# Attention and a bilinear FFN on one core: the order of 4,367 operations from a fixed table instead of a list rule

## The chip, the cores and the metric

The kernel runs on one core of one Trainium2 chip. The metric is the device time of one execution in microseconds (us), and the figure compared is the median over several runs. The notation is that of the profile: PE is TensorE's matmul side and PEld its weight loads, DVE is VectorE, ACT is ScalarE, POOL is GpSimd, and SP is SyncE, which only issues DMAs here.

## What is computed

Eight batches of twelve heads (448 positions, head width 64) go through attention with RMS-normalised queries and keys. The result, seen as a 3584 x 768 matrix, goes through a bilinear feed-forward network. All of it is in fp32.

```python
q_n, k_n = rmsnorm(q, g_q), rmsnorm(k, g_k)
scores = scale * np.matmul(q_n, k_n.transpose(0, 1, 3, 2))
attn = softmax(scores)
x = np.matmul(attn, v).transpose(0, 2, 1, 3).reshape(B * S, H * D)
out = (x @ w_a) * (x @ w_b) @ w_out
```

## The kernel before

**Attention** is cut into 24 steps, p = 0 to 23, each of four heads of one batch (three steps make a batch). For each p, three loads bring q, k and v (SP queue). `normalize` squares q and k on ACT (L458), sums them on DVE (L460), raises the mean to the power -0.5 on POOL (L466) and scales q on DVE (L470). `transposes` turns k and q on PE (L496) into a PSUM tile, and ACT copies each result to SBUF (L501 for k, L503 for q). Then come seven slices j of the keys. `scores(p, j)` is a product on PE in 64x64 tiles (L517) followed by two exponentials on ACT (L523). `values(p, j)` multiplies them with v on PE (L539). The denominators are summed on PE: for p < 5 slice by slice (`sums_over_keys`, L575), from p = 5 on after DVE and POOL have added the slices (`add_up`, L553). `invert` copies the denominators to SBUF on ACT (L588), sends one row to 112 partitions by DMA, takes the reciprocal on DVE (L608), writes it to DRAM and reads it back spread over all partitions (three transfers on the SP queue, called few, inv and rec below), and `divide` (L646) multiplies the result with it. `put_out` (L635) moves the products out of PSUM on ACT.

**Buffers.** Scores, transposed q and k and, from p = 5 on, the denominators share two PSUM buffers, tag "sc". Exponentials have four SBUF buffers, q one, k one, v two, and the spread reciprocals one ("rec").

**The network** uses a fast matrix-product scheme of seven products per 2x2 block. Its weights are prepared at the start in 18 sets (`factors`): ACT issues two loads and takes an absolute value (L271), DVE rounds (L272 to L278) and combines (L394), ACT issues the store of the result ("keep", L401 and L405). Batches are taken in pairs, beta = 0 to 3. For beta 0 and 1, `quarter_products` makes 7 products of three matmuls each for every (m, ab) (L1202). For beta 2 and 3, `deep_products` goes one level deeper (L779). `last_product` multiplies with w_out (L903, and L1100 for the deeper form `inner_products`). On the full array a matmul in the program is two records in the trace, and so is one in 64x64 tiles: a `scores`, `values` or `sums_over_keys` operation is 8 records, a transpose operation 7, a quarter product 6, half a last product 6.

**What sets the order.** Nothing is issued while the functions above run. Each calls `op`, which records an operation in a list: its engine, a planned duration, a key (a due place: lower goes first), a function that emits the instructions, what it depends on, its PSUM or SBUF tiles, and on PE its mode, "quad" for 64x64 tiles or "full". `Plan.run` then walks through time: for each engine it finds the operations that could begin within a short window (0.2 us on PE, 0.05 us elsewhere), takes the one with the lowest key, moves that engine's clock by the planned duration, and so on. It emits the operations in the order in which they were chosen. Each engine runs its own instructions in the order in which they were emitted; waits between engines are by semaphores. The planned durations and keys therefore decide only the order.

Of the kernel before, what the change touches and what calls it, by code (L numbers as in the profile page):

```python
# [24 lines left out]

class Plan:
# [9 lines left out]
    TURN = 0.18  # L36
    LANES = 8
    RATE, LANDING = 300.0, 2.0
    STAY = 0.3
    LAG = 0.1  # L40
# [31 lines left out]
    def run(self):  # L72
        ops = self.ops
        links, first = {}, {}
        for n, o in enumerate(ops):
            if o[6] is not None:
                links.setdefault(o[6], []).append(n)
        for c in links.values():
            for n in c:
                first[n] = c[0]  # L80
        users, need, left, last = {}, {}, {}, {}
        for n, o in enumerate(ops):
            head = first.get(n, n)
            outer = {d for d in o[4] if first.get(d, d) != head}
            need[head] = need.get(head, 0) + len(outer)
            for d in outer:
                users.setdefault(d, []).append(head)
            for t in o[9]:
                left[t] = left.get(t, 0) + 1
        ready = {n: 0.0 for n in need}  # L90
        opened, free, modes, cands, dma, port = {}, {}, {}, {}, 0.0, 0.0
        for n, k in need.items():
            if k == 0:
                cands.setdefault(ops[n][0], []).append(n)

        def members(n):
            return links[ops[n][6]] if ops[n][6] is not None else [n]

        def buffers(n):

            t, taken = 0.0, {}
            for x in members(n):
                for name in ops[x][8]:
                    tag, bufs = self.tags[name]
                    had = opened.setdefault(tag, [None] * bufs)
                    since = [(last.get(o, 0.0), k) for k, o in enumerate(had) if (tag, k) not in taken.values() and not left.get(o)]
                    if not since:
                        return None
                    t, taken[name] = max(t, min(since)[0]), (tag, min(since)[1])
            return t, taken  # L110

        order, end, sent = [], {}, [0.0] * self.LANES
        while any(cands.values()):
            best = None
            for e, cs in cands.items():
                f = free.get(e, 0.0) if e else 0.0
                at = {}
                for n in cs:
                    t = buffers(n)
                    if t is not None:  # L120
                        t = t[0]
                        turn = self.TURN if ops[n][5] != modes.get(e) else 0.0
                        if e == "PE" and modes.get(e) == "quad" and turn:
                            turn += self.STAY
                        at[n] = max(f, ready[n], t, port if ops[n][10] else 0.0,
                                    sent[ops[n][11] - 1 - self.LANES] if ops[n][11] else 0.0) + turn
                if at:
                    t = min(at.values()) + (0.2 if e == "PE" else 0.05)
                    n = min((n for n in at if at[n] <= t), key=lambda n: (ops[n][2], n))
                    t = at[n] - (self.STAY if e == "PE" and modes.get(e) == "quad" and ops[n][5] != "quad" else 0.0)  # L130
                    if best is None or t < best[0]:
                        best = t, e, n
            t, e, n = best
            cands[e].remove(n)
            for name, (tag, k) in buffers(n)[1].items():
                opened[tag][k] = name
            for x in members(n):
                if ops[x][5] != modes.get(e) and x != n:
                    t += self.TURN
                modes[e] = ops[x][5]  # L140
                order.append((t, x))
                t += ops[x][1]
                end[x] = t
                if ops[x][10]:
                    port = max(port, t)
                if ops[x][7]:

                    dma = max(dma, t) + ops[x][7] / self.RATE
                    end[x] = dma + self.LANDING
                    sent += [end[x]] * ops[x][11]  # L150
                for name in ops[x][9]:
                    left[name] -= 1
                    last[name] = max(last.get(name, 0.0), end[x])
                for u in users.get(x, ()):
                    ready[u] = max(ready[u], end[x] + (self.LAG if ops[u][0] != e else 0.0))
                    need[u] -= 1
                    if need[u] == 0:
                        cands.setdefault(ops[u][0], []).append(u)
            if e:
                free[e] = t  # L160
        assert len(order) == len(ops)
        self.times = order, end
        for _, n in order:
            if ops[n][3] is not None:
                ops[n][3]()


# [3 lines left out]
def kernel(  # L171
# [35 lines left out]
    nc = tc.nc  # L207
# [91 lines left out]
    def fast_body(ld, wk, ps_s, ps_o, ps_mm, dram):  # L299
# [27 lines left out]
        def rounding(key, size, get, x, w):  # L327

            for e, n, emit, r, wr in round_steps(get):
                rate = {"ACT": 950, "DVE": 1900 if n == 1 else 950, "POOL": 420}[e]  # L330
                names = {"x": x, "w": [w]}
                op(e, 0.17 + size / rate, key, emit, sum((names[c] for c in r), []), sum((names[c] for c in wr), []),
                   lock=e != "ACT")
# [25 lines left out]
        def factors(n, key, early, after):  # L359
# [30 lines left out]
            for pool_, to, x, y in steps:  # L390
                add = to == 4 and not last
                e = FACTOR if pool_ else "DVE"
                op(e, 1.05 if e == "POOL" else 0.6, key,
                   lambda e=e, to=to, x=x, y=y, add=add: two[e].tensor_tensor(  # L394
                    sts[n][:, to], sts[n][:, x], sts[n][:, y], ALU.add if add else ALU.subtract),
                   [f"{st}/{homes[x]}", f"{st}/{homes[y]}"], [f"{st}/{homes[to]}"], lock=True)
# [44 lines left out]
        def normalize(p):  # L441
# [8 lines left out]
            def squares(s, nm):  # L450
# [8 lines left out]
                op("ACT", 1.07, key, square, [f"{nm}{p}"], [sq], new=[sq])  # L459
                op("DVE", 1.1, key, lambda: nc.vector.tensor_reduce(rs[p][:, s], xs["sq", nm, p], AX, ALU.add), [sq], [f"{ms}/{nm}"])  # L460

            def roots(a, b, names):
                msf = lambda: rs[p][:, a:b].rearrange("p s n -> p (s n)")
                op("DVE", 0.2, key, lambda: nc.vector.tensor_scalar(msf(), msf(), 1.0 / D, 1e-6, ALU.mult, ALU.add), [], names)  # L464
                op("POOL", 2.7 if b - a == 1 else 5.0, key,
# [20 lines left out]
        def transposes(p):  # L486

            qkT, key = tile_of(f"qkT{p}", "qkT", 2), p - EARLY
            for n, nm in ((1, "k"), (0, "q")):
# [17 lines left out]
                op("ACT", 1.05 if n else 1.15, key, take, [pt, "gain"], [f"{qkT}/{n}"], new=[qkT] if n else [])  # L507

        def scores(p, j):
# [17 lines left out]
            op("ACT", 1.12, p, exps, [sc, f"ms{p}/k"], [E], new=[E])  # L527
# [15 lines left out]
        def add_up(p, j):  # L543
# [10 lines left out]
            op(e, 2.2 if e == "POOL" else 1.12, p, emit, [f"E{p}.{j}"] + ([f"E{p}.0"] if j == 1 else []), [t],  # L554
# [163 lines left out]
        def deep_products(beta, key, names, h):  # L718
# [12 lines left out]
            for f, x in enumerate(xs_of):  # L731
# [4 lines left out]
                for n, a, b in ((0, lambda t=token: t(0, 1), lambda t=token: t(0, 0)), (1, lambda t=token: t(1, 1), lambda k=block: k(0)),  # L736
# [6 lines left out]
                    op("DVE", 0.32, -0.4, emit, [f"{x}/0", f"{x}/1", "ended" if beta == ONCE else f"{h}/open"] + ([nm] if n else []),  # L743
# [5 lines left out]
            def step(m, f, F, names_F):  # L749
# [21 lines left out]
                def product(nm, to, terms, reads, new=None, more=False):  # L771
# [9 lines left out]
                    op("PE", len(terms) * HS / 595, key + 0.1 * (7 * m + f), emit, reads + [slot], [nm, "ffn"],  # L781
# [19 lines left out]
                def wide(to, other):  # L801
                    take("DVE", 1.02, lambda: V.tensor_tensor(F[to], F[to], F[other], ALU.add), allF(other), allF(to), lock=True)  # L802

                def times(g, i, n):
                    e = "DVE" if m == MH - 1 and f > 4 else TIMES
                    take(e, 1.2 if e == "POOL" else 0.63,
# [19 lines left out]
                take("DVE", 0.66, lambda: V.tensor_tensor(  # L826
# [36 lines left out]
        def last_product(beta, h, key):  # L863
# [48 lines left out]
            def add(to, x, t, names_in, names_out):  # L912

                return lambda po, ps: op("DVE", 0.6, -1, lambda: nc.vector.tensor_tensor(to(), x(), ps(), ALU.add),
                                         [po] + names_in, names_out)

            def out_(t, i, x, y):
# [3 lines left out]
                def take(po, ps):  # L921
# [5 lines left out]
                    op("DVE", 0.6, -1, emit, [po, f"{fin}/{'cU'[y]}{t}"], [o_sb], new=[o_sb])  # L927
# [41 lines left out]
            def plain(t, base, to):  # L969
# [3 lines left out]
                if not isinstance(to, tuple):  # L973
                    return lambda po, ps: op("DVE", 0.6, -1, lambda: nc.vector.tensor_tensor(acc(t, to), acc(t, base), ps(), ALU.add),
                                             [po, name(base)], [name(to)])

                def take(po, ps):
                    out_(t, *to[:2], base)(po, ps)
                    if len(to) > 2:
                        op("DVE", 0.6, -1, lambda: nc.vector.tensor_tensor(acc(t, to[2]), acc(t, to[2]), ps(), ALU.add),  # L980
                           [po], [name(to[2])])
# [76 lines left out]
        def inner_products(beta, key, f, group, a, base, to, acc, names, out_place):  # L1058
# [31 lines left out]
            def product(bank, x, y, reads, start, stop):  # L1090
# [11 lines left out]
                op("PE", MI * HI / 595, key, emit, reads, [nm, "ffn"], new=new, mode="full")  # L1102
# [83 lines left out]
        def quarter_products(beta, key, m, ab, st, at, names, h):  # L1186
# [42 lines left out]
            if ab == 0:  # L1229
                take("DVE", 0.68, lambda: V.tensor_tensor(fresh("U", "U", 1), C(0, 0), PS("b"), ALU.add), [b_, hp[0]], [U], [U])  # L1230
            else:
                take("DVE", 0.68, lambda: V.tensor_tensor(fresh("U", "U", 1), held["t1"], PS("b"), ALU.add), [b_, t1], [U], [U])
# [3 lines left out]
            else:  # L1236
                take("DVE", 0.68, lambda: V.tensor_tensor(C(0, 0), C(0, 0), PS("a"), ALU.mult), [a], [hp[0]])
            d = product("d", 4, B12, True, False)
            if ab == 0:
                take("DVE", 0.68, lambda: V.tensor_tensor(C(1, 1), held["U"], PS("d"), ALU.add), [d, U], [hp[1]])  # L1240
# [251 lines left out]
```

## Time and profile before

| | us |
|---|---|
| median of 3 runs | 1521.26 (1517.19 to 1521.43) |
| the profiled execution, its own time | 1517.54 |
| its span (first to last instruction) | 1515.7 |
| PE busy | 1477.4 |
| DVE busy | 1009.6 |
| ACT busy | 441.2 |
| POOL busy | 324.7 |

Stages in the profiled execution, read off the trace by which operations PE runs: from 0 to 228 us attention p = 0 to 10 with the weights being prepared; to 380 us the first network part of beta 0 alone; to 480 us attention p = 10 to 14 between parts of beta 0; to 725 us the network of beta 0 and 1; to 920 us attention p = 15 to 23 between last products of beta 1; from 920 us to the end the network of beta 2 and 3.

A row of the windows view has the stretch and its length, and then, engine by engine, the busy time and the number of instructions; the last three figures are the granted TensorE clock as a share of full speed, the mean busy share of the DMA engines, and GB/s. A row of the timeline has the start, the duration, the engine, the line, the operation, what it writes and reads, how many records are merged, and in brackets how long the engine had been idle and what ended that. A row of the waits view has who waited for whom, the total in us, how often, and the longest.

### The profile page before, as it was taken

The numbers are of one execution on the slowest core, as the hardware profiler recorded it, in microseconds if no ns is written. First come the engines' busy times: TensorE is split into PE (matmuls) and PEld (weight loads), VectorE is DVE, ScalarE is ACT, GpSimd is POOL, SyncE is SP. The second block draws the span as 40 slices with busy tenths as digits, with TensorE's granted clock in tenths as the row PEclk, the third lists the DMA queues.
The fourth block names the chain that finished last, engine by engine and source line by source line (L and its number), as shares of the span: only waits on it lengthen the run. The fifth ranks groups of instructions, "written<-read, shape, count | busy, mean of one in ns | idle before, by whom it ended". The sixth has DMA issues, their size and how long they took to land.

```text
span 1515.7 us, 21017 instructions
## 1 busy us (share of the span) xinstructions
PE 1477.4 (97%) x7854; PEld 981.6 (65%) x7854; DVE 1009.6 (67%) x1568; ACT 441.2 (29%) x790; POOL 324.7 (21%) x172
## 2 busy tenths in 40 slices
PE   8998999999999999999999999999999999999998
PEld 5553345555445555555544445699997889999798
DVE  5887869888784233343667656477777667777785
ACT  6777661111554000000177761011111011111000
POOL 3426442111241001000265541011210001211000
PEclk9999999999999999999999999999999999999999
DMA  9897455554532464555656534655555755554554
GB/s 274 247 283 194 99 111 181 189 200 156 156 109 75 130 191 136 167 177 182 184 134 169 119 115 123 186 156 157 157 157 187 254 165 158 157 157 135 197 172 118
DMA packets 189074, 250.73 MB, mean 165 GB/s; under 512 B 61988, under 2 KB 160804, under 8 KB 182308
## 3 DMA queue, kind: packets, MB, share of 16 engines
q1 hardware_dynamic: 160900, 195.82, 45.5%
q10 hardware_dynamic: 28064, 53.48, 10.0%
q8 instruction: 64, 1.05, 0.3%
q14 instruction: 46, 0.38, 0.1%
HBM read 191.10 MB, written 57.97 MB: 164 GB/s over the span
## 4 chain that ended last, share of the span: by engine, by line
PE 86%; DMA 6%; DVE 3%; ACT 2%; issue 1%; SPq 1%; ACTq 0%; DVEq 0%
PE pq L1202 25%; PE dg L779 17%; PE po L903 15%; PE da L779 6%; PE o L539 6%; PE sc L517 6%; PE g L1100 2%; PE a L1100 2%; PE pt L496 2%; DMA q_sb<-in_q_dram 2%; PE su L575 1%; ACT ET L523 1%; PE b L1100 1%; DMA kept_o<-st 1%; PE d L1100 1%
## 5 line engine op out<-in xcount | busy, mean ns | idle before, releaser
L1202 PE MATMUL pq<-x,st 128*128 128x448 f32 x1008 | 382.4, 541 | 0.0
L1202 PEld LDWEIGHTS pq<-x,st 128*128 128x128 f32 x1008 | 190.8, 190 | 188.7 <-issue 181.7
L523 ACT ACTIVATE ET<-sc,ms 128x448 f32<-128x448 f32 x336 | 192.3, 632 | 86.5 <-PE sc L517 71.1
L539 PE MATMUL o<-ET,v_sb 64*64 64x448 f32 x1344 | 192.5, 546 | 3.6 <-ACT ET L523 2.9
L517 PE MATMUL sc<-qkT 64*64 64x448 f32 x1344 | 180.0, 543 | 16.3 <-ACT ET L523 9.1
L466 POOL TENSOR_TENSOR ms<-ms,expo 128x14 f32<-128x14 f32 x48 | 151.3, 3154 | 176.2 <-DVE ms L464 175.6
L779 PE MATMUL dg<-x,st 128*128 128x224 f32 x672 | 169.6, 355 | 2.0 <-DVE dF L826 2.0
L779 PE MATMUL dg<-dT,st 128*128 128x224 f32 x672 | 168.3, 353 | 1.9 <-DVE dt L819 1.9
L903 PE MATMUL po<-st,hT 128*128 128x384 f32 x492 | 163.4, 488 | 0.0
L807 POOL TENSOR_TENSOR hT<-dF 128x448 f32<-128x448 f32 x42 | 47.6, 1143 | 427.3 <-DVE dF L802 427.3
L903 PEld LDWEIGHTS po<-st,hT 128*128 128x128 f32 x492 | 92.9, 190 | 66.9 <-issue 6.0
L779 PEld LDWEIGHTS dg<-x,st 128*128 128x128 f32 x672 | 126.5, 190 | 5.3 <-DVE dF L826 5.3
L779 PEld LDWEIGHTS dg<-dT,st 128*128 128x128 f32 x672 | 126.7, 190 | 3.2 <-DVE dt L819 2.8
L779 PE MATMUL da<-x,st 128*128 128x224 f32 x504 | 123.2, 353 | 1.1 <-ACT dt L792 1.1
L517 PEld LDWEIGHTS sc<-qkT 64*64 64x64 f32 x1344 | 60.7, 133 | 89.6 <-issue 35.5
L539 PEld LDWEIGHTS o<-ET,v_sb 64*64 64x64 f32 x1344 | 61.3, 132 | 81.1 <-ACT ET L523 42.3
L553 POOL TENSOR_TENSOR sum<-sum,ET 128x896 f32<-128x896 f32 x38 | 81.1, 2134 | 104.0 <-ACT ET L523 60.8
L779 PEld LDWEIGHTS da<-x,st 128*128 128x128 f32 x504 | 93.0, 190 | 4.5 <-ACT dt L792 2.1
L802 DVE TENSOR_TENSOR dF<-dF 128x896 f32<-128x896 f32 x84 | 93.3, 1111 | 3.4 <-DVE dF L831 0.5
L792 ACT COPY dt<-da 128x224 f32<-128x224 f32 x84 | 29.1, 346 | 209.2 <-PE da L779 209.2
L553 DVE TENSOR_TENSOR sum<-sum,ET 128x896 f32<-128x896 f32 x57 | 62.0, 1088 | 38.2 <-POOL sum L553 34.0
L903 PE MATMUL po<-st,fin 128*128 128x384 f32 x252 | 86.7, 492 | 0.0
(136 smaller groups left out, 1683.6 us busy)
## 6 DMA issues: line engine op xcount, KB each, us to landing
st<-kept_o SPq DMA_DIRECT2D x28, 1152.0 KB
st<-kept_s SPq DMA_DIRECT2D x84, 320.0 KB
kept<-st ACTq DMA_DIRECT2D x12, 1344.0 KB
st<-kept SPq DMA_DIRECT2D x12, 1344.0 KB
st<-kept SPq DMA_DIRECT2D x84, 192.0 KB
ti<-kept_t SPq DMA_DIRECT2D x48, 288.0 KB
kept_s<-ds SPq DMA_DIRECT2D x30, 448.0 KB
q_sb<-in_q_dram SPq DMA_DIRECT2D x48, 224.0 KB
```

What stands on the lines that cost most here:

```text
L466: lambda: nc.gpsimd.tensor_tensor(msf(), msf(), expo[:, 0:2 * NT * (b - a)], ALU.pow), [], names)
L496: nc.tensor.transpose(t[:, j * P:(j + 1) * P], x[:, j].rearrange("p h d -> p (h d)"), ident)
L517: nc.tensor.matmul(t[low_high[w], e, 0:S], lhsT=qkTs[p][low_high[e], 1, j * P + w * D:j * P + (w + 1) * D], rhs=qkTs[p][low_high[e], 0, w ...
L523: nc.scalar.activation(E[:, e], scs[p, j][:, e, 0:S], AF.Exp, scale=rs[p][:, 1, 2 * j + e:2 * j + e + 1])
L539: nc.tensor.matmul(os_[p][low_high[e], w, 0:S], lhsT=xs["v", p][low_high[w], e, j * D:(j + 1) * D], rhs=ETs[p, j][low_high[w], e], start=( ...
L553: two[e].tensor_tensor(sums[p], sums[p] if j > 1 else ETs[p, 0], ETs[p, j], ALU.add)
L779: nc.tensor.matmul(to(), lhsT=W(w), rhs=t(), start=not more and k == 0, stop=k == len(terms) - 1, skip_group_check=True)
L802: take("DVE", 1.02, lambda: V.tensor_tensor(F[to], F[to], F[other], ALU.add), allF(other), allF(to), lock=True)
L807: lambda: two[e].tensor_tensor(C(i, n), F[g][:, 0:S], F[g][:, S:2 * S], ALU.mult), allF(g),
L903: nc.tensor.matmul(held["po"][:, 0:HALF], lhsT=a[0]()[:, c], rhs=sts[beta, 12 + place_of[f]][:, c], start=(c == 0), stop=(c == MH - 1))
L1100: nc.tensor.matmul(held[bank], lhsT=x()[:, c], rhs=y(c), start=(start and c == 0), stop=(stop and c == MI - 1), skip_group_check=True)
L1202: nc.tensor.matmul(banks[bank][:, 0:S], lhsT=sts[at][:, f, c * P:(c + 1) * P], rhs=quads[x][:, c], start=(start and c == 0), stop=(stop an ...
```

## The change

The body of `Plan.run` is replaced. In place of the walk through time there is a table, `ORDER`, a packed list of 4,367 places. Step k takes the operation at place `places[k]` of those not yet emitted, checks that all it depends on has been emitted, and emits it.

```diff
-            t, e, n = best
-            cands[e].remove(n)
...
-        for _, n in order:
-            if ops[n][3] is not None:
-                ops[n][3]()
+        n = len(ops)
+        places = zlib.decompress(base64.b85decode(ORDER))
+        assert len(places) == 2 * n
+        rest, at = list(range(n)), {}
+        for k in range(n):
+            x = rest.pop(places[k] + 256 * places[n + k])
+            assert all(d in at for d in ops[x][4])
+            at[x] = k
+            if ops[x][3] is not None:
+                ops[x][3]()
```

Many planned durations change too, for example

```diff
-                op("ACT", 1.07, key, square, [f"{nm}{p}"], [sq], new=[sq])
+                op("ACT", 0.95, key, square, [f"{nm}{p}"], [sq], new=[sq])
```

and so do the constants of `Plan` (`TURN` from 0.18 to 0.13, `LAG` from 0.1 to 0.04, and new ones). The new `run` reads none of them: it uses only an operation's dependencies and its emitting function. Operations, tiles, buffer counts and DMAs are the same in both kernels.

The table can be decoded and laid beside the order that the rule of before gives. How many operations stand at another place of their engine's own queue:

| engine | operations | moved | furthest, places |
|---|---|---|---|
| PE | 1450 | 343 | 10 |
| DVE | 1566 | 1176 | 39 |
| ACT | 678 | 342 | 18 |
| POOL | 164 | 93 | 15 |
| SP | 455 | 373 | 58 |

On PE every move lies in the attention stages; behind the last `sums_over_keys` (920 us in the profile) PE's order is the same. PE changes between quad and full mode 105 times in the order of before (counting the first) and 93 times in the table. As an example, PE's queue around p = 6 (S is `scores`, V `values`, U `sums_over_keys`, T a transpose of k or q, with p and j behind S and p behind the others; V's slices come in the order of S's):

```
before: S6.0 S6.1 U5 V6 S6.2 V6 S6.3 V6 S6.4 V6 S6.5 V6 S6.6 V6 Tk7 Tq7 V6 S7.0 S7.1 V7 S7.2 U6 V7 S7.3
table:  S6.0 S6.1 S6.2 V5 S6.3 U5 V6 S6.4 V6 V6 S6.5 V6 V6 S6.6 V6 Tk7 Tq7 V6 S7.0 S7.1 S7.2 S7.3 U6 V7 S7.4
```

## The prediction

> **What bounds the kernel now.** I read the page first, then busy time by stage, then PE's own waits, then PE's timeline where it stalls, last the chain of waits. The page's first part and the windows:
>
> ```profile
> PE 1477.4 (97%) x7854; PEld 981.6 (65%) x7854; DVE 1009.6 (67%) x1568; ACT 441.2 (29%) x790; POOL 324.7 (21%) x172
> ```
> ```profile
> 0.00:114.00 114.00, 104.06 (x956) 63.27 (x957) 89.29 (x108) 80.16 (x121) 40.59 (x20) 1.00 0.95 269
> 114.00:228.00 114.00, 103.12 (x799) 45.62 (x798) 83.61 (x97) 78.79 (x128) 59.59 (x24) 1.00 0.56 133
> 228.00:380.00 152.00, 152.00 (x405) 76.85 (x404) 133.61 (x155) 23.93 (x25) 26.92 (x17) 1.00 0.51 181
> 480.00:725.00 245.00, 245.00 (x680) 129.34 (x680) 87.86 (x123) 10.07 (x20) 16.95 (x15) 1.00 0.52 161
> 725.00:920.00 195.00, 191.26 (x1396) 91.96 (x1395) 131.31 (x184) 120.84 (x200) 98.93 (x39) 1.00 0.56 141
> 920.00:1516.00 596.00, 582.11 (x2926) 528.44 (x2922) 414.20 (x820) 69.66 (x199) 47.57 (x42) 1.00 0.55 167
> ```
>
> PE is the bound, at full clock. Where only the network runs (228 to 380, 480 to 725) it never stops; no order can help there. In the first 228 us it stands still 20.8 us, though DVE (76%) and ACT (70%) have room: these are waits of order, not of capacity. The DMA engines are nearly full (0.95) in the first 114 us.
>
> A stall costs more than its idle time, because a restarted matmul shows its whole latency as busy. So I summed, over PE's 7,854 records, the time from start to start less the back-to-back interval of the form. The intervals come from rows such as these of the chain:
>
> ```profile
> 227.75 158.11 PE pq L1202 x420
> 479.46 62.12 PE po L903 x192
> ```
>
> 158.11 / 420 = 0.376 us, 62.12 / 192 = 0.323 us; likewise 0.189 us for 224 columns, 0.163 for 192, 0.109 for a transpose, and 0.75 us for the eight records of a 64x64 operation. At these intervals all records take 1425.0 us; 82.9 us are **lost between starts**: 6.7 before 14 us, 14.7 to 114, 22.4 to 228, 0 to 380, 6.8 to 480, 0 to 725, 18.0 to 920, 14.3 after. How it is lost in the two attention stages:
>
> ```profile
> 73.47 1.74 PE L517 MATMUL sc<-qkT 64*64 64x448 f32 x16 [1.14 <-ACT qkT L503]
> 75.58 1.12 PE L539 MATMUL o<-ET,v_sb 64*64 64x448 f32 x5 [0.37 <-ACT ET L523]
> ```
> ```profile
> 137.18 0.93 PE L517 MATMUL sc<-qkT 64*64 64x448 f32 x8
> 137.93 0.93 PE L539 MATMUL o<-ET,v_sb 64*64 64x448 f32 x8
> 139.39 0.98 PE L517 MATMUL sc<-qkT 64*64 64x448 f32 x8 [0.52 <-ACT ET L523]
> 140.19 0.93 PE L539 MATMUL o<-ET,v_sb 64*64 64x448 f32 x8
> 141.65 0.98 PE L517 MATMUL sc<-qkT 64*64 64x448 f32 x8 [0.52 <-ACT ET L523]
> ```
>
> First row: scores wait 1.14 us for ACT's copy of the transposed q, as nothing stands between. Second: values wait for exponentials. Below: the denominators of step 5 hold one of the two "sc" buffers from 135.6 us until ACT copies them at 147.0, and scores go through the other one by one: 2.26 us a round (139.39 to 141.65) for 1.5 us of work.
>
> **The skill.** The Trainium skill, "Trainium Kernel Development and Optimization", Performance Expectations, says that matmul busy time is a bad metric for the distance to the best, as matmuls are pipelined; the trace agrees (97% busy, yet 82.9 us, 5.5%, lost). "TensorEngine Tiling (Array Packing)", Key Properties, says that changing the tiling mode drains TensorE; here the last 64x64 record to a full-array one takes 0.466 us where the next 64x64 group takes 0.354, and full to 64x64 takes 0.093 more than its interval: about 0.1 us a turn. "PSUM — Partial Sum Buffer", Engine vs sequencer instructions, says that ScalarE, VectorE and GpSimd queues are strict first in, first out: a misplaced instruction holds all behind it. "DMA: Bandwidth & Descriptors", Issuing engines are not separate DMA queues, says that transfers from all issuers share 16 engines; the trace has a q load landing after 9.30 us (issued 121.58) amid weight loads.
>
> **The change part by part.** The order is known before any run: I decoded the table and laid it beside the rule's order. From it I take positions alone; durations are the trace's.
>
> *Planned durations*: nothing, they are no longer read. *Operations, DMAs, waits*: the same number of each; no new wait exists, only other places in the queues.
>
> *Turns on PE*: 105 to 93, 12 x 0.1 = **1.2 us** gained, all on the path.
>
> *PE's places in attention.* An exponential pair is done about 1.5 us after its scores leave the array (139.39 + 0.75 to 141.65), so two 64x64 operations must stand between. I counted, over all 24 steps, places with too little between (by the intervals above): values behind their scores with less than 1.4 us of PE work: 12 before, **0** in the table. Scores that need a buffer whose exponentials had less than 1.4 us: 14 and **5**. Scores behind the q transpose with nothing between: 4 and **1**. Scores issued while denominators hold a buffer: 28 and **16**. Of 30 bare places (the first three kinds) 24 go. Values with just two operations between fall from 78 to 19: slack for ACT's queue. The cover is other attention work, or a piece of the network that was there anyway.
>
> By stage, in us:
> - 14 to 114: 14.7 lost, 0.9 of it turns (9). 6 of 8 bare places go, but this stage also waits on DMA and DVE. I take 8 of 13.8.
> - 114 to 228: 22.4, 2.0 turns (20). 10 of 14 bare places go. I take two thirds of 20.4: 13.5.
> - 380 to 480: 6.8, 2.6 turns (26): 2.5 of 4.2.
> - 725 to 920: 18.0, 4.8 turns (48). All 7 bare places go, but many small waits remain: 8 of 13.2.
> - After 920 PE's order is the same. DVE's wait-makers move: the factor of the block at 1454 us (PE waits 1.8 us) stands six places earlier in DVE's queue. The four waits near 1 us at the start and end of each deep part come from PE's own order and stay. 2 of 14.3.
> - Before 14 us: loads, the norm and POOL's power chain set it; 0.
>
> With the turns: 8 + 13.5 + 2.5 + 8 + 2 + 1.2 = **35.2 us**.
>
> *Moves on ACT, DVE, POOL and SP* (342, 1176, 93, 373 operations) are the price, not shown by this trace, so bounded: at best 0 (all work hidden behind PE); at worst they give all of it back (a rival). Queued behind a misplaced store ("keep") or denominator copy on ACT are the exponentials, and PE waits for those within 1.5 us. Counts to the same landmarks hardly differ (weight loads on ACT's queue ahead of step 5's first exponentials: 16 before, 15 in the table), so DMA pressure is the same per step but in less time. One place I can price: the first product that needs step 5's combined block (at 171 us) comes through denominators copied at 147.0, three transfers, divide and combine, done at 165.4: 18.4 us. In the table that product stands some 14 us of PE work behind the copy. I take 4 us here and 2 elsewhere: **-6**.
>
> Sum: 35.2 - 6 = 29 us. DVE must then do its 172.9 us of the first 228 in some 206: 84%, still not the bound. The profiled execution (1517.54) would become 1488; the median of the three runs is 3.7 above it. From the median: 1521.3 - 29 = **1492 us**, likeliest range 1482 to 1502.
>
> **Rivals.**
> 1. *Round trips through DMA set the pace of a step.* q has one buffer: load (9.3 us when DMA is full), square 0.95, sum 1.08, power 3.15, scaling 1.09 make 15.6 us a step before queueing, where PE's own work for p < 5 is 17.4 us (21 x 0.75 + 14 x 0.109 + turns). The denominators' trip from 170.8 to 182.4 is 11.6 us, and "rec" has one buffer. For: the chain of waits runs through these transfers. Against: PE's waits name ACT, hardly DMA (1.4 us). If they take the place of half the gain: 1521 - 14 = 1507, with 1502 to 1516.
> 2. *Slower: ACT's queue blocked by denominator copies.* The table fixes where each copy stands among the exponentials; if "rec" comes free later than its place, exponentials behind it wait, and PE with them. Price: the trace has 5.2 us of this wait in 6 places, 1.2 at most. It decides once it passes 35 / 24 = 1.5 us per step beyond what the copies cost now, in all 24 steps; at 2 us a step the kernel takes 1521 + 48 - 35 = 1534.
> 3. *Nothing*: the PE places are filled but the waits move on to exponentials, ACT being busy 70% of the first 228 us. Then 1521 within 5 us. Against: the other 30% is room. That the table does not reach the chip can't be: each engine takes emitted order.
> 4. *Better than I allow*: few new waits and three quarters of the 51 us of non-turn loss in attention go: 38 + 1.2 for turns + 2 after 920, 1521 - 42 = 1479.
>
> **How the numbers follow.** Forecast 0.50, rival 1 0.25, rival 4 0.10, nothing 0.08, slower 0.07. The measurement can tell about 0.3% (4.6 us). Faster: 0.50 + 0.10 + 0.25 = 0.85; same 0.08; slower 0.07. The range reaches up through rival 1 and down past rival 4's centre: 1476 to 1514.
>
> **What would show it.** PE's idle time in the first 228 us' worth of work falls from 20.8 to under 10 us; step 6's rounds of 2.26 us go to 1.5; waits of scores on L503 and L523 (15.2 us on PE) halve; time between starts lost in all falls to about 54 us; the stretches of pure network keep their lengths. Wrong would be: new PE waits on DMA or on DVE's combine over 10 us, longer waits of ACT's denominator copies, or the stage after 920 us changed by over 5 us.

## The result, and the profile after

The kernel with the table is slower: 1598.11 us, median of 6 runs (1594.04 to 1600.98), against 1521.05 us for the kernel before (6 runs, 1517.19 to 1522.87). The ratio is 1.0506, 95% interval 1.0488 to 1.0525. The time lies outside the predicted range, on the other side of no change.

The profiled execution after took 1594.04 us, span 1592.2. Lines of the kernel after are those of before less 32 (L779 is now L747, L819 is L787). The page's first part, then the rows of the windows for attention's start and for the part from 920 us:

```profile
PE 1489.2 (94%) x7854; PEld 953.4 (60%) x7854; DVE 980.5 (62%) x1568; ACT 438.9 (28%) x790; POOL 318.5 (20%) x172
```
```profile
0.00:114.00 114.00, 100.81 (x928) 49.00 (x928) 85.93 (x106) 78.79 (x119) 36.47 (x19) 0.99 0.90 253
114.00:228.00 114.00, 106.94 (x845) 46.57 (x842) 83.76 (x106) 81.44 (x132) 65.32 (x24) 1.00 0.58 147
920.00:1592.00 672.00, 594.49 (x2892) 517.65 (x2890) 391.64 (x796) 67.60 (x197) 46.90 (x42) 0.99 0.48 147
```

The clock is full, DVE, ACT and POOL are busy for less time than before, and PE for only 11.8 us more. The last stage is 76 us longer with 12.4 us more of busy PE: 77.5 us of idleness where there were 13.9. The first two stages hold as much idleness as before (20.3 us; it was 20.8). Because stage borders shift, I compared the start of the same PE operation in both traces:

| PE reaches | before | after | gained since the row above |
|---|---|---|---|
| values of p = 5 | 118.2 | 120.4 | -2.2 |
| values of p = 11 | 394.2 | 395.7 | 0.7 |
| values of p = 20 | 850.2 | 847.0 | 4.7 |
| first deep product, beta 2 | 972.4 | 962.4 | 6.8 |
| its last products | 1149.5 | 1188.9 | -49.4 |
| first deep product, beta 3 | 1228.9 | 1269.0 | -0.7 |
| its last products | 1405.5 | 1483.9 | -38.3 |
| end of the span | 1515.7 | 1592.2 | 1.9 |

Attention gained 10.0 us in all. The two stretches of deep products lost 87.7. PE's waits after:

```profile
PE dg L747 <- DVE dt L787: 49.5, 46, 2.3
PE dg L747 <- DVE dt L786: 8.7, 15, 1.0
PE sc L485 <- ACT qkT L471: 6.2, 7, 2.1
PE pt L464 <- ACT ET L491: 5.4, 3, 2.7
PE dg L747 <- DVE dF L794: 4.3, 12, 0.8
PE da L747 <- ACT dt L760: 4.3, 6, 1.1
PE sc L485 <- ACT ET L491: 2.9, 5, 0.6
```

And the rows of before that bear on these:

```profile
PE sc L517 <- ACT ET L523: 9.1, 15, 1.5
PE sc L517 <- ACT qkT L503: 6.1, 9, 1.2
PE dg L779 <- DVE dt L819: 1.9, 2, 1.0
```

The scores' waits for exponentials fell from 9.1 to 2.9 us. Their waits for the copy of q did not fall: three of the four longest of before are gone, but two longer ones have come, 1.45 us at 134.43 and 2.10 us at 787.34. The top two rows of after are for the two DVE additions into dt of a deep step, and before they came to 1.9 us in 2 places. For what follows, four names within a deep step, by the code printed above: the *first products* go to columns of bank 0 of the tile dg; the two *adds* (L786, L787) read them; the two *second products* go to bank 1; the *third product* accumulates into bank 1, and the *last add* (L799) reads it. One step of before and one of after in the timeline, without the rows of weight loads, ACT and DMA issues:

```profile
1057.42 0.92 PE L779 MATMUL dg<-dT,st 128*128 128x224 f32 x4
...
1058.18 0.92 PE L779 MATMUL da<-x,st 128*128 128x224 f32 x4
1058.45 0.39 DVE L818 TENSOR_TENSOR dt<-dt,dg 128x224 f32<-128x224 f32 x1 [0.48 <-PE dg L779]
1058.87 0.39 DVE L819 TENSOR_TENSOR dt<-dt,dg 128x224 f32<-128x224 f32 x1
1058.94 0.92 PE L779 MATMUL dg<-x,st 128*128 128x224 f32 x4
...
1059.69 0.54 PE L779 MATMUL dg<-dT,st 128*128 128x224 f32 x2
1059.89 0.39 DVE L831 TENSOR_TENSOR dF<-dt,dg 128x224 f32<-128x224 f32 x1 [0.63 <-PE dg L779]
```
```profile
1046.72 0.92 PE L747 MATMUL dg<-dT,st 128*128 128x224 f32 x4
...
1048.24 0.92 PE L747 MATMUL dg<-x,st 128*128 128x224 f32 x4
...
1049.19 0.39 DVE L799 TENSOR_TENSOR dF<-dt,dg 128x224 f32<-128x224 f32 x1 [1.97 <-PE dg L747]
1049.50 0.38 DVE L786 TENSOR_TENSOR dt<-dt,dg 128x224 f32<-128x224 f32 x1
...
1049.91 0.39 DVE L787 TENSOR_TENSOR dt<-dt,dg 128x224 f32<-128x224 f32 x1
...
1050.35 0.65 PE L747 MATMUL dg<-dT,st 128*128 128x224 f32 x2 [1.20 <-DVE dt L787]
```

Before, the adds run at 1058.45, while PE works on the product to da, and are done by 1059.26, ahead of the second products (1059.69). After, in the table's order the last add of the step before (L799) stands ahead of them in DVE's queue. It waits 1.97 us for the third product of its own step, so the adds, ready since about 1047.6, start at 1049.50, and PE, with its second product next, stands 1.20 us.

Why does PE wait at all? A second product reads nothing that the adds write, and it writes a bank that they don't read. In the built program of each kernel a second product waits for an add only where the add was emitted ahead of it; where the add is emitted behind it, the add waits for the product instead. The two share the tile dg, and the ordering on that tile follows the order of emission; the experiments test this. The plan names the halves of dg apart (`gb`, `gg`), so this wait is in neither its dependencies nor its model. The rule emits the adds ahead of both second products in 82 of the 84 deep steps, and early in DVE's queue. The table puts the last add of the previous step ahead of the second of the two adds in 57 of 82 neighbouring step pairs (of the first as well in 25). In 68 of the 84 steps it emits at least one add ahead of a second product, and in 16 both behind both. By start-to-start intervals (the prediction's measure of lost time) the second products lose 74.6 us (2.6 before) and the third 8.2 (3.9).

### The profile page after: what moved, and what is told of

Its sections match the earlier page's. It is cut to its first block, busy times and chain, and to the rows that moved or that the text cites. A ratio compares the mean times of both kernels' runs of the same rounds, so it can differ in the third digit from the quotient of the medians.

```text
span 1592.2 us, 21039 instructions
## 1 busy us (share of the span) xinstructions
PE 1489.2 (94%) x7854; PEld 953.4 (60%) x7854; DVE 980.5 (62%) x1568; ACT 438.9 (28%) x790; POOL 318.5 (20%) x172
## 5 line engine op out<-in xcount | busy, mean ns | idle before, releaser
L747 PE MATMUL dg<-dT,st 128*128 128x224 f32 x672 | 175.3, 363 | 58.3 <-DVE dt L787 49.5
L747 PE MATMUL dg<-x,st 128*128 128x224 f32 x672 | 169.9, 355 | 4.4 <-DVE dF L794 4.3
L434 POOL TENSOR_TENSOR ms<-ms,expo 128x14 f32<-128x14 f32 x48 | 145.6, 3037 | 133.9 <-DVE ms L432 133.5
L747 PEld LDWEIGHTS dg<-dT,st 128*128 128x128 f32 x672 | 122.7, 190 | 80.2 <-DVE dt L787 65.5
L485 PE MATMUL sc<-qkT 64*64 64x448 f32 x1344 | 157.1, 549 | 9.7 <-ACT qkT L471 6.2
L507 PE MATMUL o<-ET,v_sb 64*64 64x448 f32 x1344 | 153.4, 540 | 0.6 <-ACT ET L491 0.6
L747 PEld LDWEIGHTS dg<-x,st 128*128 128x128 f32 x672 | 125.6, 190 | 10.4 <-DVE dF L794 9.5
L747 PE MATMUL da<-x,st 128*128 128x224 f32 x504 | 125.0, 357 | 5.1 <-ACT dt L760 4.3
L485 PEld LDWEIGHTS sc<-qkT 64*64 64x64 f32 x1344 | 47.2, 133 | 95.2 <-issue 43.1
L747 PEld LDWEIGHTS da<-x,st 128*128 128x128 f32 x504 | 93.2, 191 | 12.0 <-ACT dt L760 9.6
L507 PEld LDWEIGHTS o<-ET,v_sb 64*64 64x64 f32 x1344 | 53.1, 133 | 72.1 <-issue 59.4
L786 DVE TENSOR_TENSOR dt<-dt,dg 128x224 f32<-128x224 f32 x84 | 32.4, 385 | 84.4 <-PE dg L747 84.2
```

The source lines that it names most:

```text
L434: lambda: nc.gpsimd.tensor_tensor(msf(), msf(), expo[:, 0:2 * NT * (b - a)], ALU.pow), [], names)
L485: nc.tensor.matmul(t[low_high[w], e, 0:S], lhsT=qkTs[p][low_high[e], 1, j * P + w * D:j * P + (w + 1) * D], rhs=qkTs[p][low_high[e], 0, w ...
L507: nc.tensor.matmul(os_[p][low_high[e], w, 0:S], lhsT=xs["v", p][low_high[w], e, j * D:(j + 1) * D], rhs=ETs[p, j][low_high[w], e], start=( ...
L747: nc.tensor.matmul(to(), lhsT=W(w), rhs=t(), start=not more and k == 0, stop=k == len(terms) - 1, skip_group_check=True)
L786: take("DVE", 0.38, lambda: V.tensor_tensor(part(1), part(0), bank(0, 0)(), ALU.add), [gb, tt], [tt])
```

## Experiments

Theory A is the one just given. Theory B puts the loss on DVE's queue alone, theory C on what the new attention part leaves behind when the deep part begins. In all these kernels both orders are kept as tables, `table` and `rule`, and a third is made of them; none leaves out any computation. The first, second, fourth and fifth ran on one chip beside the kernel before at 1519.08 us, the others on another beside 1517.89 us; each ratio is to the kernel before on the same chip. The first and the fourth can't tell A from B, since both expect the same there; the second and the fifth can.

**The rule's order from the first deep product on.**

```diff
+    head = head[:next(k for k, x in enumerate(head) if first in plan.names[x])]
+    there = set(head)
+    return head + [x for x in tail if x not in there]
```

Here `head` is the table, `tail` the rule's order and `first` the first deep product, "da2.0.0".

> The table's order up to the first product of the deep part (da2.0.0, 974 us in the changed kernel), the rule's order from there. Theory A (in the deep part the emitted order decides which of two engines waits: TensorE's products into the second bank of a 'dg' tile wait for VectorE's adds out of its first bank when those were emitted earlier, and the adds wait for products emitted earlier; the table puts the adds between the two products): the 85 us lost behind da2.0.0 come back, 10 us of attention gain stay: 1511 us. Rival B (VectorE's own queue order in the deep part is to blame, whatever the emitted order): the same 1511. Rival C (the deep part is late because of transfers or buffers that the attention stages left behind): most of the loss stays, above 1560.

Measured: 1510.82 us (1509.08 to 1512.69), ratio 0.9944 (0.9927 to 0.9960). C falls: the loss lies in the order from the first deep product on. The rest of the table is a gain of some 8 us, and this kernel is faster than both. Its waits in the deep part are those of before:

```profile
PE dg L801 <- DVE dF L848: 2.0, 2, 1.0
PE dg L801 <- DVE dt L841: 1.9, 2, 1.0
```

**Only the order of emission changed.** Every engine's queue is exactly that of before; the adds are emitted between the two second products.

```diff
+            before += [(second[0], adds[0]), (adds[1], second[1])]
+    return merged(plan, rule, queues_of(plan, rule), before)
```

> The rule's order: every engine's queue exactly as in the kernel before. Only the emitted order between engines differs: in each of the 84 deep steps the two adds are emitted between the two products, so that the adds wait for the first product and the second product waits for the adds. A: 84 waits of about 1 us each, 1595 to 1610 us. B and C: 1521.

Measured: 1628.95 us (1628.51 to 1634.33), ratio 1.0734 (1.0712 to 1.0756). No instruction moved in any queue, and the kernel is 110 us slower. Of all pairs of operations on different engines that share a tile, only 164 were emitted in the other order: in 82 steps the two adds and the one second product (in the first step of each deep part the rule had them so already). One step, without weight loads and ACT, and the row of the waits:

```profile
1062.40 0.54 PE L838 MATMUL dg<-x,st 128*128 128x224 f32 x2
1063.05 0.39 DVE L877 TENSOR_TENSOR dt<-dt,dg 128x224 f32<-128x224 f32 x1 [2.70 <-PE dg L838]
1063.47 0.39 DVE L878 TENSOR_TENSOR dt<-dt,dg 128x224 f32<-128x224 f32 x1
...
1063.91 0.65 PE L838 MATMUL dg<-dT,st 128*128 128x224 f32 x2 [0.97 <-DVE dt L878]
```
```profile
PE dg L838 <- DVE dt L878: 81.9, 84, 1.3
```

The wait comes in each of the 84 deep steps. The adds wait for the one second product and the other waits for the adds: two handovers in each step. Idleness is 0.98 us a time, but from start to start the second products lose 104.4 us and the third 10.5. A's mechanism holds; its size was too low, since it counted the idleness alone (1595 to 1610 us were expected). B and C can't explain this run.

**The tile declared as two.** In the kernel just shown, the buffer of every third deep step (`turn == 1`) is declared as two tiles of one bank each, in place of one of two banks.

```diff
-                            held["g"] = (ps_o if turn == 1 else ps_s).tile([P, 2, 512], FP32, tag=home[0], name="dg")
+                            held["g"] = two_banks("dg") if turn == 1 else [ps_s.tile([P, 2, 512], FP32, tag="sc", name="dg")]
...
+        def two_banks(name):
+            return [ps_o.tile([P, 512], FP32, tag=f"o{n}", name=name) for n in range(2)]
```

The other users of that buffer, attention's values among them, get the two tiles as well.

> The kernel with every queue as before and only the adds emitted between the two products (1628.95 us, every step's second product waiting for the add), with one thing changed: the buffer of 2 x 512 words that every third deep step takes is declared as two buffers of one bank each, in the same place and of the same total size. Theory A (the wait is one on the buffer as a whole, although the product writes a bank that the add doesn't read): in those 28 of 84 steps the wait is gone and in the other 56 nothing changes. In the run without the split the steps of each of the three kinds lost 35 us before that product, so 1594 us (1588 to 1600), and PE's row of waits for the second add falls from 84 times to about 56. Rival D (the two are in each other's way in the memory itself, or the order in which the operations are emitted changes something else): 1622 to 1635, and the loss of 35 us in those steps stays.

Measured: 1591.97 us (1590.45 to 1597.16), ratio 1.0500 (1.0483 to 1.0516), as A said.

```profile
PE dg L843 <- DVE dt L883: 54.7, 56, 1.3
```

28 of the 84 waits are gone, those of the split steps. By kind of step, the second products lose 35.0, 0.0 and 34.7 us, where without the split they lost 35.0, 34.7 and 34.7. So it is the declaration of the tile, not the memory, that makes PE wait. This agrees with the Trainium skill, "PSUM — Partial Sum Buffer", PSUM bank collisions raise a hardware error, whose rule in its simple version is to guard PSUM by bank. In two of the split steps a second product even runs beside an add out of the other bank, which happens in no step of the unsplit kernels; one of them:

```profile
1178.13 0.39 DVE L883 TENSOR_TENSOR dt<-dt,dg 128x224 f32<-128x224 f32 x1
1178.18 0.54 PE L843 MATMUL dg<-dT,st 128*128 128x224 f32 x2
```

**The table with the adds ahead.** In DVE's queue the adds go ahead of the last add of the previous step (`r`), and both are emitted ahead of the second products, as the rule does it.

```diff
+            if q.index(r) < q.index(adds[1]):
+                q[:] = [x for x in q if x not in adds]
+                q[q.index(r):q.index(r)] = adds
+        before += [(adds[1], second[0]) for adds, _, second in part]
```

> The table everywhere; in the deep parts alone, each step's two adds into dt move ahead of the last add of the step before where the table had them behind it (181 of VectorE's 1566 places), and are emitted ahead of both products. A and B: the waits of those products (74 us between starts) go, about 1515 to 1525 us. C: no change, 1598.

Measured: 1517.86 us (1513.33 to 1525.86), ratio 0.9993 (0.9982 to 1.0004): 80.3 us of the difference from the kernel with the table (1598.11) are back, of the 86.5 that it lost from the first deep product to the end. In the profile (of the longest of the 20 runs, 1525.86 us) PE still waits for adds in 11 places:

```profile
PE dg L842 <- DVE dt L882: 10.1, 11, 1.8
```

**The table's queues with the adds emitted late.** Every queue as in the kernel with the table; both second products are emitted ahead of the adds, so that they don't wait.

```diff
+            before += [(second[1], adds[0])]
+    return merged(plan, table, queues_of(plan, table), before)
```

> The table: every engine's queue exactly as in the changed kernel. Only the emitted order differs: in each of the 84 deep steps both products are emitted ahead of the adds, so that TensorE does not wait for the adds there, and the adds wait for both products. A: the 74 us of waits on the adds go, but the adds end later and some third products (which wait for the adds' reader) become late by some tenths of a us: 1525 to 1550. B: 1598 or more. C: 1598.

Measured: 1588.11 us (1586.85 to 1590.03), ratio 1.0450 (1.0433 to 1.0468). A was right on the wait and wrong on the time. The second products now lose 2.5 us, but the products to da lose 44.1 (9.6 in the kernel with the table) and the third products 37.9 (8.2), and the waits have moved:

```profile
PE da L838 <- ACT dt L851: 24.7, 32, 2.5
PE dg L838 <- DVE dF L885: 23.8, 45, 1.4
```

The adds now wait for the second products and are later still. What needs their result (the addition into dF at L885, then PE's third product; ACT's copies of later da) comes late in their place. So B has its part: the table's place of the adds in DVE's queue is itself too late. The loss needs adds that end late, by their place in the queue as here or by a wait for a product as in the second experiment, and a product on PE that waits for them or for what follows from them. With the table's queues, turning the wait round hands the loss on: 10 of 79 us came back.

**Where attention's gain went.** By start-to-start intervals up to 970 us, from before to after: values and scores together lose 38.0 and then 15.2 us, but transposes 11.5 and 17.4, full-array products 15.4 and 19.3, the rest 2.9 and 5.6. That is 22.8 gained and 12.5 given back. The largest stall that is new, after (DVE, ACT's DMA queue, ACT, PE):

```profile
70.03 0.25 DVE L576 RECIPROCAL few<-few 112x16 f32<-112x16 f32 x1 [4.24 <-DMA few<-rec]
70.20 0.49 DVE L362 TENSOR_TENSOR st<-st 128x384 f32<-128x384 f32 x1
...
70.73 0.55 ACTq L370 DMA_DIRECT2D kept_o<-st  x1
71.32 2.21 ACT L491 ACTIVATE ET<-sc,ms 128x448 f32<-128x448 f32 x4 [4.64 <-DVE st L362]
```
```profile
72.53 0.98 PE L464 MATMUL pt<-ident,k_sb 128*128 128x128 f32 x7 [2.66 <-ACT ET L491]
```

DVE's reciprocal waits 4.24 us for the denominators' transfer; a weight combination behind it could have run. ACT's store of those weights waits for that, the exponentials behind the store wait with it, and PE loses 2.66 us. Two kernels, on top of that of the first experiment, the fastest so far, move what blocks. One moves the reciprocal of p = 1 four operations later on DVE, and ACT's square of q of p = 5 (3.41 us behind a load) two later; the other only ACT's store, behind the exponentials.

```diff
+    return later(plan, from_here(plan, table, rule), [("DVE", "few1", 4), ("ACT", "sqq5", 2)])
...
+    return later(plan, from_here(plan, table, rule), [("ACT", "kept16", 2)])
```

> The fastest so far (1510.82 us) with two instructions later in their engine's queue, PE's queue untouched: DVE's reciprocal of pair 1 (it waited 4.27 us for a DMA at 64.9 to 69.1 us, and ACT's store, the exponentials and PE's transposes stood behind it, PE for 2.71 us) 4 operations later, and ACT's square of q of pair 5 (3.41 us for its load at 90.9 us, PE 2.24 us behind it) 2 operations later. Theory A (what the table's order missed of its gain in the first stages was lost to instructions at the head of a queue that wait for a DMA, with work behind them that was ready): both of PE's waits fall under 0.6 us and the time to 1506.5 us (1505 to 1508). Rival B (PE was to lose this time anyway; other waits take the place of these): 1510 to 1512.

> The fastest so far (1510.82 us) with one instruction moved: ACT's store of the combined weights, which stood 4.7 us in ACT's queue behind DVE's blocked combination, goes behind the four exponentials that followed it. DVE's reciprocal stays where it is and waits as before. Theory A (the exponentials were late because ACT's queue was blocked by that store, not because their own inputs were late): PE's wait of 2.71 us at 71.6 us falls under 0.6, DVE's wait of 4.27 us stays, 1508.3 us (1507 to 1509.6). Rival B (PE stands behind DVE by another way, or loses the time in the next wait): 1510 to 1512.

Measured: 1509.14 us (1504.95 to 1514.44), ratio 0.9949 (0.9931 to 0.9967), and 1510.27 us (1506.01 to 1516.75), ratio 0.9954 (0.9939 to 0.9968). The first lies between the two forecasts, but neither ratio can be told from 0.9944. The stalls they aimed at are gone in both profiles. Others stand in their place, in the first:

```profile
78.03 1.16 DVE L718 TENSOR_TENSOR x<-x,rec 128x448 f32<-128x448 f32 x2 [3.16 <-DMA rec<-inv]
79.27 0.53 ACT L660 COPY rec<-su 128x448 f32<-128x448 f32 x1 [3.39 <-DVE x L718]
...
79.85 1.41 PE L647 MATMUL su<-ET,ones 64*64 64x448 f32 x8 [2.19 <-ACT rec L660]
```

and in the second:

```profile
76.59 1.60 ACT L343 ACTIVATE st<-lraw 128x1536 f32<-128x1536 f32 x1 [3.27 <-DMA kept_o<-st]
...
78.77 1.40 PE L611 MATMUL o<-ET,v_sb 64*64 64x448 f32 x5 [2.90 <-ACT ET L595]
```

B held. In the first profile, PE came to the denominators of the next slices (L647) earlier and stood there for ACT's copy, which needs the one "rec" buffer, which the division frees, which waits for the transfer back. The division of p = 1 ends at 79.2 us here and at 80.0 us without the moves, and 1.3 us of start lies between these two profiles (first values at 17.0 and 18.3 us). In the second, ACT comes to the next weights' absolute value (L343) some 4 us earlier than without the move, at 73.3 us, and stands there until the store of the last ones has landed and freed their buffer, at 76.6 us. Both fit a round trip through DMA that sets the pace, so that a stall ahead of it costs little of what it shows; no run here made such a trip shorter, so this is not shown.

**The rule's order also for the first 120 us.** The table is left for the transposes of p = 5 to the first deep product.

```diff
+    return from_here(plan, from_here(plan, rule, table, "ptk5"), rule)
```

> The fastest so far (table up to the first deep product, then the rule's order: 1510.82 us) with the rule's order also for the first 120 us, so the table only from the transposes of pair 5 to the first deep product. The first 120 us are where the table lost 2 to 3 us against the rule (values of pair 5 at 121.3 us instead of 118.2), and the later stages where it gained. Theory A (the two stretches are independent of each other): 1508 us (1506 to 1510). Rival B (the later gain needs the places that the earlier part leaves, or the order of the two parts doesn't fit where they meet): 1511 or more.

Measured: 1504.30 us (1501.73 to 1507.78), ratio 0.9912 (0.9898 to 0.9925), the fastest of all, and below the 1506 to 1510 that A expected. The side of A was right; its reason was only partly so. Values of p = 5 start at 120.4 us, 0.9 ahead of the kernel that it is compared with, and most of the rest came in stretches whose order is the same in both (14.7 to 12.0 us lost from 120 to 228 us, 15.3 to 12.9 from 730 us to the first deep product). Whether the earlier part hands over DVE and the queues in a better state, or part of this is the difference between single profiles, is open.

## Why the prediction was wrong

- **The bound**: right. PE stayed the bound at full clock, and lost time between starts is the difference: 82.9 to 158.2 us, 75.3 more, of 76.5 us of span.
- **The step that failed**: "After 920 PE's order is the same", with 2 us of gain, and above it "no new wait exists, only other places in the queues". I counted how many places operations had moved on DVE, 1,176, and looked at one of them at 1454 us (that one did come as said: its 1.8 us wait is gone). I took waits to be part of the operations. The runs showed that between two operations that share only a tile the order of emission decides who waits, and the kernel with every queue unchanged lost 110 us by that alone. Late places in DVE's queue had their part, as the fifth experiment shows. The term of +2 measured -86.5 (from the first deep product to the end of the span: 543.3 us before, 629.8 after).
- **What the profile could have shown**: the wait itself. In the first step of each deep part of before, PE's second product stands for an add that it doesn't read:

```profile
976.42 0.39 DVE L819 TENSOR_TENSOR dt<-dt,dg 128x224 f32<-128x224 f32 x1
976.86 0.65 PE L779 MATMUL dg<-dT,st 128*128 128x224 f32 x2 [0.96 <-DVE dt L819]
```

  These are two of the "four waits near 1 us" that the prediction put down to PE's own order. In the step shown above from the middle of the part the adds end at 1059.26 us and the second products start at 1059.69: 0.43 us of slack, and as much in the median step. So there were 82 more steps in which this wait was met just in time, in a table where L831 had moved ahead of L819 in 57.
- **Attention**: mis-sized in time. Values waiting on exponentials nearly vanish, and the scores' waits on q's copy and exponentials fall from 15.2 to 9.1 us, not quite half. All of that fall is in the exponentials; the bare places behind q's transposes were filled (4 to 1), but the waits for q's copy came elsewhere (6.1 and 6.2 us). The terms 8 + 13.5 + 2.5 + 8 + 1.2 less 6 are 27.2 us; the measured gain is 10.0. By the intervals above the places gained 22.8 us, where these terms come to 33.2 without the 6, and 12.5 us were given back, where 6 had been taken for the moves on ACT, DVE and SP. Idleness in the first two stages was to fall under 10 us and stayed at 20.3.
- **Rivals**: the first (round trips through DMA) fits attention best, with 10 us left where it gave 14, but it was not put to a test of its own. The second, slower by ACT's denominator copies, had the right sign for the whole and the wrong place, so its sign came true by luck: PE's waits for these copies come to 3.0 us in all (1.1 before), 1.6 of them at 150.84 us. The loss had no rival of its own.
- **Its own sign of error** came true: the stage after 920 us changed by over 5 us.

## What to carry to other kernels

When the order of operations is changed by hand or by search, list the pairs of operations on different engines that share a tile without sharing data, and either declare the parts as tiles of their own, where they lie in different banks as here, or keep the order of such pairs; a model that lacks these waits gives no reason to keep it. Moving an instruction that waits on a DMA behind work that is ready removed its stall in the two kernels that tried it, and gained nothing that could be measured: another wait took its place. A wait that the profile shows in only two places may have been met just in time in all the others, so read its slack off the timeline.

## What the runs showed that I had not expected

The same instructions in the same queues, emitted in another order, took 1519 and 1629 us, by nothing but the direction of the waits on one tile in 82 deep steps. A handover from PE to DVE and back cost 0.98 us of idleness in each deep step, and 104.4 / 84 = 1.24 us between starts. Undoing two stalls of 2.71 and 2.24 us on PE took the time from 1510.82 to 1509.14 us, and the ratio to the kernel before from 0.9944 to 0.9949, a difference within the intervals of the two.
